# One place in each unit for ScalarE's part of a weight conversion, and an earlier Newton step, in an attention and two-MoE kernel

## The chip, the cores and the metric

The kernel runs on one core of one Trainium2 chip. The metric is the device time of one execution in microseconds. Before the change the median of three runs is 876.39 us (876.0 to 878.66).

## What is computed

The reference chains three layers. First comes attention over 4 batches of 8 heads, 576 positions and head size 64, in which a position sees itself and the 63 positions in front of it. Then a gated layer over the 2304 tokens (512 features, 1536 hidden), with a root-mean-square norm in front of it. Last comes a layer of eight experts, of which each token takes the one with the largest gate.

```python
rms = np.sqrt(np.mean(x * x, axis=-1, keepdims=True) + 1e-06)
xn = x / rms * rms_g
g = xn @ w_gate
silu = g * (1.0 / (1.0 + np.exp(-g)))
val = xn @ w_val
return (silu * val @ w_out).astype(np.float32)
```

The arrays `w_gate`, `w_val` and `w_out` of the second layer come to the chip in float64, because dividing by a NumPy float64 scalar turns them into that type. The kernel brings them to float32 on the chip; this conversion is what the change is about.

## The kernel before

**Stages.** In the page's times: attention to about 130 us, the gated layer to about 600 us, the experts behind it. All five engines run through written-out instruction streams, in the order in which the Python program issues them (`manual_schedule`); nothing is reordered afterwards. Each engine works its stream in order, and waits where an operand isn't ready.

**The gated layer.** Its weights are cut into 12 columns `f` of 128 hidden features (`wraw[f]`, 1536 numbers in each partition: 512 of gate, 512 of value, 512 of out). The tokens are cut into blocks (`BLOCKS`); the first has two sub-blocks of 384 tokens. A *unit* `u` is one column with one sub-block, so the first block has units 0 to 23: an even unit and the odd one behind it share a column, but for units 0 to 3. For each unit TensorE makes gate and value (`gate_val`, 48 matmuls into two banks), and then the output product of the unit before (`out_b`, 9 matmuls). ScalarE makes the silu of the gate into `t` (L642), VectorE multiplies it by the value (L643), ScalarE casts the product to the high half `hh` (L644), and the low half `hl` is a subtraction, on GpSimd in the first block (L645). The banks of gate and value are the same two for all units from 2 on, so that the next unit's gate needs this unit's L642, and its value this unit's L643. Every matrix is split in such a way into a high and a low half of float32r, and each product is three matmuls.

**Weights of a unit.** `w_split` casts a column's high half on ScalarE (L546) and subtracts for the low half (L548). For gate and value (`wha`, `wla`) this is done two units ahead of an even unit, with the subtraction on VectorE; for the out part (`who`, `wlo`) one unit ahead, in an odd unit, with the subtraction on GpSimd.

**The conversion.** `w_conv` turns a column of float64 into float32 in two *halves* of 768 numbers; half `i` belongs to column `i // 2`. A DMA (L389, `w_load`) brings the words of a half into one of three buffers `st`. For halves from 4 on, the steps are:

- ScalarE, `inside(i)`: the sign and the range of each number in `gt` (two buffers), by L458 and L459.
- ScalarE, `scaled(i)`: the high word times 65536 into the place of the result in `wraw`, L466.
- VectorE: shift and mask in place (L427), the low word's bits put in (L432), and the minimum with the largest float32 and the product with the sign (L440).

Half `i` must be through before the cast of its column. `w_conv` is a generator that yields its estimated cost; `beside` runs pieces of it, of the norms and of later work behind each unit until that unit's budget (`BUDGET`) is used up, and `convert` makes it run on where a column is needed. In the kernel before, VectorE's piece of half `i` issues ScalarE's two steps of half `i + 1` between L432 and L440 (`if i + 1 in st_t:`), so that ScalarE works ahead; the first two pairs of `inside` are issued in two of the last steps of attention (`if g in (NG + 1, NG + 2) and w64`).

**The norms.** `norm(i)` prepares the tokens of sub-block `i`: a DMA of the attention's output into `xr` (L323), squares on ScalarE (L332), sums (L337), a sum over partitions on TensorE (`ones`), three Newton steps for the inverse root (each is a square on ScalarE, L355, and L357 and L359 on VectorE), and for four chunks a scaling (L366, VectorE), a cast (L368, ScalarE) and a subtraction (L371, VectorE) into `xt`. Norm 1 belongs to the second sub-block, used from unit 2 on; norms 2 and later belong to the next blocks and run beside the units of the first.

**The end of attention.** In the steps behind the last group of heads, ScalarE and VectorE copy the last results out of their banks (L248, L249). Unit 1 takes two of these banks.

**SyncE's queue** issues all the loads above in program order, together with eight writes of 1 MB that fill `xs` for the experts, one in every second unit from unit 2 on (L916).

Of the kernel before, what the change touches and what calls it, by code (L numbers as in the profile page):

```python
# [22 lines left out]
NF = FF // 128  # L23
# [27 lines left out]
def attention_moe_moe_kernel(ctx, tc, qT, kT, vw, w1p, rms_g, wg2, wg2T, w2p, out):  # L51
# [67 lines left out]
    w64 = w1p.dtype != F32  # L119
# [52 lines left out]
    NG = NU * 3  # L172
# [101 lines left out]
    def beside(tasks, budget):  # L274

        for t in tasks:
            t.rest = 0.0
        while budget > 0:
            can = [t for t in tasks if not t.done and t.rest <= 0 and t.want != "bank"
                   and not (callable(t.want) and not t.want())]  # L280
            if not can:
                break
            cost = can[0].piece()
            budget -= cost
            for o in tasks:
                if o is not can[0]:
                    o.rest -= cost
        return budget
# [88 lines left out]
    st_t, freed = {}, []  # L377
# [13 lines left out]
    def w_conv(f):  # L391


        for h in range(2):
            if not w64:
                w_load(2 * f + h + 3)
                continue
            i = 2 * f + h
            gt = inside(i)
            wf = half(i)  # L400
            w = wf.bitcast(I32)
            if f < 2:
                st = st_t.pop(i)
                lo, hi = st[:, :, 0], st[:, :, 1]
                nc.vector.tensor_scalar(out=w, in0=hi, scalar1=3, scalar2=0x3FFFFFFF,
                                        op0=ALU.logical_shift_left, op1=ALU.bitwise_and)
                yield 0.55
                while freed:
                    w_load(freed.pop())
                nc.vector.scalar_tensor_tensor(out=w, in0=lo, scalar=29, in1=w,  # L410
                                               op0=ALU.logical_shift_right, op1=ALU.bitwise_or)
                yield 1.0
                nc.vector.scalar_tensor_tensor(out=w, in0=hi, scalar=-0x40000000, in1=w,
                                               op0=ALU.bitwise_and, op1=ALU.bitwise_or)
                yield 1.0
                if i + 1 in st_t and i < 3:
                    inside(i + 1)
                del in_t[i]
                yield "rest"
                nc.vector.scalar_tensor_tensor(out=wf, in0=gt, scalar=TINY64 * TINY64, in1=wf,  # L420
                                               op0=ALU.is_ge, op1=ALU.mult)
                yield 0.9
            else:
                scaled(i)
                yield 0.0
                lo = st_t.pop(i)[:, :, 0]
                nc.vector.tensor_scalar(out=w, in0=w, scalar1=3, scalar2=0x7FFFFFFF,  # L427
                                        op0=ALU.logical_shift_left, op1=ALU.bitwise_and)
                yield 0.6
                while freed:  # L430
                    w_load(freed.pop())
                nc.vector.scalar_tensor_tensor(out=w, in0=lo, scalar=29, in1=w,  # L432
                                               op0=ALU.logical_shift_right, op1=ALU.bitwise_or)
                yield 1.2
                if i + 1 in st_t:
                    inside(i + 1)
                    scaled(i + 1)
                del in_t[i]
                yield "rest"
                nc.vector.scalar_tensor_tensor(out=wf, in0=wf, scalar=FMAX, in1=gt,  # L440
                                               op0=ALU.min, op1=ALU.mult)
                yield 1.0
            freed.append(i + 3)

    in_t, sc_t = {}, set()

    def half(i):
        return wraw[i // 2][:, i % 2 * HW:(i % 2 + 1) * HW]
# [1 line left out]
    def inside(i):  # L450

        if i not in in_t:
            gt = in_t[i] = gt_p.tile([P, HW], F32, name="gt")
            hi = st_t[i][:, :, 1].bitcast(F32)
            if i < 4:
                nc.scalar.activation(gt, hi, AF.Square, scale=1.0)
            else:
                nc.scalar.activation(gt.bitcast(I32), hi, AF.Copy, scale=0.49 / TINY64)  # L458
                nc.scalar.activation(gt, gt.bitcast(I32), AF.Sign, scale=1.0)  # L459
        return in_t[i]  # L460

    def scaled(i):

        if i not in sc_t:
            sc_t.add(i)
            nc.scalar.activation(half(i), st_t[i][:, :, 1].bitcast(F32), AF.Copy, scale=65536.0)  # L466
# [85 lines left out]
    for g in range(NG + LV):  # L552
        if g == NG:
            early.finish()
            norm0.finish(bank[2])
        if g < NG:
            if g % 3 == 0:
                qk_load(g // 3 + 2)
            if g % 3 == 2:
                v_load(g // 3 + 1)  # L560
            scores(g)
        if 0 <= g - LT < NG:
            transposes(g - LT)
        if 0 <= g - LV < NG:
            pv(g - LV)
        if g >= NG:
            for _ in range(2):
                next(first_gv, None)
        if 0 <= g - LT < NG:
            pt_copy(g - LT)  # L570
        if 0 <= g - 2 < NG:
            normalise(g - 2)
        attending_work(g)
        if g < NG:
            softmax(g)
        if 0 <= g - LV < NG:
            xo_out(g - LV)
        if 0 <= g - 1 < NG:
            guard(g - 1)
        if g in range(G_LOAD, G_LOAD + 5, 2):  # L580
            w_load((g - G_LOAD) // 2)
        if g == 1:
            nc.sync.dma_start(table.rearrange("(p a) w -> p (a w)", p=P), fill.rearrange("p a w -> p (a w)"))
            nc.sync.dma_start(x2dram[NT:NT + 1], zrow)
        if g == NG - 1:

            nc.scalar.activation(warm, warm, AF.Silu, scale=1.0)
        elif g == NG:
            rest1 = w_split(1, ("b", 1), wraw[1], 1024, {"a": nc.gpsimd}, "a")
        elif g == NG + 1:  # L590
            for _, r in rest1:
                r()
        if g in (NG + 1, NG + 2) and w64:
            inside(g - NG + 3)
    for _ in first_gv:
        pass
    actx.close()
    attending[0] = False

# [293 lines left out]
    for u, (k, i) in enumerate(units):  # L893
        n = steps[k][0]
        first, last = (i == steps[k][2][x] for x in (0, -1))
        begin = u == starts[blocks[n][2][0]]
        gate_val(u)
        silu(u)
        budget = BUDGET[n] + min(spare, 0.5)

        if len(blocks[n][2]) > 1:
            bk = bank[1]
        else:
            bk = bank[4] if n == len(blocks) - 1 else bank[5]
        if u > 0:
            out_b(u - 1)
        if not (begin and len(blocks[n][2]) == 1):
            budget -= on_bank(bg, bk)
        if u > 0:
            budget -= evac(u - 1)  # L910
        if u == stops[i]:
            free[0] = i + 1
        if u in range(2, 2 + 2 * E, 2):

            e = u // 2 - 1
            nc.sync.dma_start(xs[e * NT:e * NT + 4 * P], x2dram[NT:NT + 1].to_broadcast([4 * P, DM]))  # L916
        rest = b_split(heads[u + 1], "o") if u + 1 in heads else []
        if u + 2 in heads:
            rest += b_split(heads[u + 2], "a")
        elif u + 2 >= len(units):  # L920
            rest += c_split(u + 2 - len(units), True)
        if conv.done and wg_bc is None:
            right.close()
            g_p, r_p, j_p = (pool(x, b, right, side="right") for x, b in (("g", 1), ("r", 2), ("j", 2)))
            wg_bc = g_p.tile([P, E, DM], F32, name="wg_bc")
            nc.sync.dma_start(wg_bc, wg2T.partition_broadcast(P))
        budget -= sum(c for c, _ in rest)
        spare = beside([norm1, conv] + bg, budget)
        for _, r in rest:
            r()  # L930
        if n == len(blocks) - 1 and last:

            while c_next < NRING and (c_next + 1) * W2B <= (NF + 2 + k - len(steps)) * WB:
                c_load(c_next)
                c_next += 1
        if u + 3 in heads:
            spare -= convert(max(f for _, f, _ in steps[:heads[u + 3] + 1]) + 1, conv)
        if u + 1 < len(units):
            while normed[0] < units[u + 1][1]:
                late = normer if norm1.done else norm1  # L940
                late.piece(bk if late.want == "bank" else None)
        bg = [t for t in bg if not t.done]
# [257 lines left out]
```

## Time and profile before

| what | value |
|---|---|
| median of three runs | 876.39 us |
| the profiled execution by itself | 877.93 us |
| its span, first to last instruction | 876.1 us |
| mean granted TensorE clock | 0.992 of full speed |
| TensorE matmul busy | 838.9 us, 96% |
| TensorE weight loads busy | 772.7 us, 88% |
| VectorE busy | 605.1 us, 69% |
| ScalarE busy | 449.7 us, 51% |
| GpSimd busy | 203.1 us, 23% |

The profile is one execution on the chip. Engines are PE (TensorE matmuls), PEld (its weight loads), DVE (VectorE), ACT (ScalarE), POOL (GpSimd) and SP (SyncE, DMA issue). Times in the rows are in us from the start of the span; L57 is the helper that issues every matmul. The shares are means over the whole span, so a stage must be looked at by itself.

### The profile page before, as it was taken

How to read it: one execution, taken by the hardware profiler on the slowest of the kernel's cores; microseconds unless marked ns; L12 is line 12 of the kernel's file. 1: busy time of each engine (PE TensorE's matmuls, PEld its weight loads, DVE VectorE, ACT ScalarE, POOL GpSimd, SP SyncE). 2: the span in 40 equal slices, each digit the busy share in tenths (PEclk: the TensorE clock that was granted, in tenths of full speed). 3: DMA queues.
4: the chain of work that ended last, by engine and by line, in shares of the span. 5: the costliest groups of instructions: out<-in, count | busy, mean ns of one | idle time of the engine just before them, and what ended most of it. 6: DMA issues, size and time to landing. Idle time of an engine off the chain costs nothing.

```text
span 876.1 us, 13526 instructions
## 1 busy us (share of the span) xinstructions
PE 838.9 (96%) x4667; PEld 772.7 (88%) x4667; DVE 605.1 (69%) x1472; ACT 449.7 (51%) x993; POOL 203.1 (23%) x227
## 2 busy tenths in 40 slices
PE   7999987999999999999999999999999999989995
PEld 7999986899999999999999999988888898878884
DVE  6789877677975667675578854697775756655463
ACT  5787786776754334222334333335655655554452
POOL 3348573322332000000500041005200121022011
PEclk9999999999999999999999999999999999999998
DMA  7988615999732210000220016424774565462010
GB/s 215 301 268 266 202 67 152 240 236 218 186 87 106 98 36 1 1 0 1 82 64 1 1 49 204 169 97 150 220 254 155 192 217 168 169 210 74 2 45 20
DMA packets 47071, 114.49 MB, mean 131 GB/s; under 512 B 10223, under 2 KB 14703, under 8 KB 46834
## 3 DMA queue, kind: packets, MB, share of 16 engines
q1 hardware_dynamic: 42386, 103.50, 38.7%
q0 software_dynamic: 4576, 9.47, 2.9%
q8 instruction: 77, 1.26, 0.6%
q14 instruction: 32, 0.26, 0.1%
HBM read 93.90 MB, written 31.10 MB: 143 GB/s over the span
## 4 chain that ended last, share of the span: by engine, by line
PE 73%; DVE 9%; issue 7%; DMA 4%; ACT 3%; POOL 2%; SPq 0%; POOLq 0%; DVEq 0%; ACTq 0%
PE bank L57 70%; DMA out_dram<-x,ix 3%; DVE junk L708 2%; DMA st<-in_w1p_dram 1%; PE bank L226 1%; PE bank L849 1%; DVE wla L548 1%; POOL wraw L221 1%; DVE t L643 1%; DVE sm L208 1%; ACT gt L458 1%; DVE wlo L548 0%; POOL out_dram L1019 0%; DVE wraw L432 0%; DVE wraw L230 0%
## 5 line engine op out<-in xcount | busy, mean ns | idle before, releaser
L57 PE MATMUL bank<-xt,wha 128*128 128x384 f32 (+3 forms) x1728 | 421.6, 328 | 18.2 <-issue 6.6
L57 PEld LDWEIGHTS bank<-xt,wha 128*128 128x128 f32 x1728 | 305.1, 189 | 34.9 <-issue 7.9
L57 PE MATMUL bank<-xt,wla 128*128 128x384 f32 (+3 forms) x864 | 281.2, 326 | 0.7 <-DVE wla L548 0.7
L57 PEld LDWEIGHTS bank<-xt,wla 128*128 128x128 f32 x864 | 163.6, 189 | 2.3 <-DVE wla L548 1.7
L57 PE MATMUL bank<-who,hl 128*128 128x512 f32 x384 | 151.8, 395 | 0.6 <-DVE hl L1003 0.6
L57 PE MATMUL bank<-wlo,hh 128*128 128x512 f32 x384 | 151.9, 396 | 0.0
L57 PE MATMUL bank<-who,hh 128*128 128x512 f32 x384 | 151.2, 394 | 0.4 <-ACT hh L644 0.2
L644 ACT CAST hh<-t 128x384 fp32r<-128x384 f32 x72 | 37.0, 513 | 149.6 <-DVE t L643 149.6
L548 DVE TENSOR_TENSOR wla<-wraw,wha 128x512 fp32r<-128x512 f32 (+1 forms) x112 | 98.9, 883 | 5.1 <-ACT wha L546 4.6
L1003 DVE SCALAR_TENSOR_TENSOR hl<-bank,hh 128x512 fp32r<-128x512 f32 (+1 forms) x72 | 45.3, 629 | 82.3 <-ACT hh L1002 82.1
L643 DVE TENSOR_TENSOR t<-t,bank 128x384 f32<-128x384 f32 x72 | 39.8, 553 | 85.0 <-PE bank L57 75.7
L1002 ACT ACTIVATE hh<-bank 128x512 fp32r<-128x512 f32 (+1 forms) x72 | 39.7, 551 | 99.4 <-PE bank L57 99.3
L57 PEld LDWEIGHTS bank<-who,hl 128*128 128x128 f32 x384 | 72.3, 188 | 17.4 <-DVE hl L1003 1.4
L546 ACT CAST wha<-wraw 128x512 fp32r<-128x512 f32 (+1 forms) x113 | 87.0, 770 | 0.0
L1019 POOL DMA_INDIRECT out_dram<-x,ix x32 | 34.9, 1091 | 217.8 <-ACT x L1018 210.8
L57 PEld LDWEIGHTS bank<-who,hh 128*128 128x128 f32 x384 | 72.8, 189 | 12.1 <-issue 0.5
L57 PEld LDWEIGHTS bank<-wlo,hh 128*128 128x128 f32 x384 | 72.6, 189 | 11.1
L57 PE MATMUL bank<-kt,qz 128*128 128x128 f32 x288 | 76.3, 405 | 5.4 <-DMA kt<-in_kT_dram 4.7
L546 ACT CAST who<-wraw 128x512 fp32r<-128x512 f32 x111 | 68.7, 619 | 20.6 <-PE bank L57 20.5
L57 PEld LDWEIGHTS bank<-kt,qz 128*128 128x128 f32 x288 | 72.4, 334 | 6.0 <-issue 4.7
L708 DVE SCALAR_TENSOR_TENSOR junk<-x,wg_bc 128x512 f32<-128x512 f32 x120 | 75.9, 686 | 0.0
L548 DVE TENSOR_TENSOR wlo<-wraw,who 128x512 fp32r<-128x512 f32 x99 | 68.1, 688 | 11.0 <-ACT who L546 6.3
(162 smaller groups left out, 959.9 us busy)
## 6 DMA issues: line engine op xcount, KB each, us to landing
wraw<-in_w2p_dram SPq DMA_DIRECT2D x64, 512.0 KB, 4.4
st<-in_w1p_dram SPq DMA_DIRECT2D x24, 768.0 KB, 6.7
wraw<-in_vw_dram SPq DMA_DIRECT2D x16, 512.0 KB, 4.4
xs<-x2dram SPq DMA_DIRECT2D x8, 1024.0 KB, 11.7
qz<-in_qT_dram SPq DMA_DIRECT2D x32, 144.0 KB, 5.5
xdram<-wraw SPq DMA_DIRECT2D x16, 288.0 KB, 2.3
x2dram<-x SPq DMA_DIRECT2D x18, 256.0 KB, 2.9
kt<-in_kT_dram SPq DMA_DIRECT2D x15, 288.0 KB, 5.9
```

Of the source, the lines that this page charges most:

```text
L57: nc.tensor.matmul(o, l, r, start=start, stop=stop)
L208: nc.vector.tensor_tensor_reduce(out=sm[:, j], in0=sb[:, j * P:(j + 1) * P], in1=mask[:, 0 if i0 + j == 0 else 1], scale=-0.125, scalar=3. ...
L221: nc.gpsimd.tensor_tensor(out=p, in0=p, in1=rs.unsqueeze(2).to_broadcast([P, 3, P]), op=ALU.mult)
L226: nc.tensor.transpose(bank[3 + g % 2][:, j * P:(j + 1) * P], p[:, j], ident)
L546: nc.scalar.copy(wh, src[:, r])
L548: e.tensor_tensor(out=wl, in0=src[:, r], in1=wh.bitcast(F32), op=ALU.subtract)))
L643: nc.vector.tensor_tensor(out=t, in0=t, in1=v, op=ALU.mult)
L644: nc.scalar.copy(hh[:, :nt], t)
L708: nc.vector.scalar_tensor_tensor(out=junk, in0=x2, scalar=1.0, in1=wg_bc[:, e], op0=ALU.mult, op1=ALU.mult, accum_out=lg[:, j, e:e + 1])
L1002: nc.scalar.activation(hh[:, :n], bank[k % 2][:, :n], AF.Relu, scale=1.0)
L1003: nc.vector.scalar_tensor_tensor(out=hl[:, :n], in0=bank[k % 2][:, :n], scalar=0.0, in1=hh[:, :n].bitcast(F32), op0=ALU.max, op1=ALU.subtract)
L1019: d = nc.gpsimd.indirect_dma_start(out=out[:, :], in_=y, in_offset=None, out_offset=bass.IndirectOffsetOnAxis(ap=ix[:, j, 0:1], axis=0), b ...
```

## The change

The diff is whole.

```diff
--- before.py
+++ after.py
@@ -396,6 +396,8 @@
                 w_load(2 * f + h + 3)
                 continue
             i = 2 * f + h
+            if f >= 2:
+                yield lambda: i in sc_t
             gt = inside(i)
             wf = half(i)
             w = wf.bitcast(I32)
@@ -432,17 +434,21 @@
                 nc.vector.scalar_tensor_tensor(out=w, in0=lo, scalar=29, in1=w,
                                                op0=ALU.logical_shift_right, op1=ALU.bitwise_or)
                 yield 1.2
-                if i + 1 in st_t:
-                    inside(i + 1)
-                    scaled(i + 1)
                 del in_t[i]
-                yield "rest"
                 nc.vector.scalar_tensor_tensor(out=wf, in0=wf, scalar=FMAX, in1=gt,
                                                op0=ALU.min, op1=ALU.mult)
+                halves[0] = i + 1
                 yield 1.0
             freed.append(i + 3)
 
-    in_t, sc_t = {}, set()
+    in_t, sc_t, halves = {}, set(), [4]
+
+    def ahead():
+
+        i = next((i for i in range(halves[0], 2 * NF) if i not in sc_t), 2 * NF)
+        if w64 and i < min(halves[0] + 2, 2 * NF) and i in st_t:
+            scaled(i)
+            inside(i)
 
     def half(i):
         return wraw[i // 2][:, i % 2 * HW:(i % 2 + 1) * HW]
@@ -585,15 +591,16 @@
         if g == NG - 1:
 
             nc.scalar.activation(warm, warm, AF.Silu, scale=1.0)
+            if w64:
+                inside(4)
         elif g == NG:
             rest1 = w_split(1, ("b", 1), wraw[1], 1024, {"a": nc.gpsimd}, "a")
         elif g == NG + 1:
             for _, r in rest1:
                 r()
-        if g in (NG + 1, NG + 2) and w64:
-            inside(g - NG + 3)
     for _ in first_gv:
         pass
+    beside([norm1], 1.2)
     actx.close()
     attending[0] = False
 
@@ -925,6 +932,10 @@
             wg_bc = g_p.tile([P, E, DM], F32, name="wg_bc")
             nc.sync.dma_start(wg_bc, wg2T.partition_broadcast(P))
         budget -= sum(c for c, _ in rest)
+        if u == 0 and w64:
+            scaled(4)
+        elif n == 0:
+            ahead()
         spare = beside([norm1, conv] + bg, budget)
         for _, r in rest:
             r()
```

ScalarE's two steps of a half are no longer issued by VectorE's piece of the half before. A new function `ahead` issues them for the next half that has not had them, once in each unit of the first block, behind the unit's weight cast and in front of the pieces that `beside` runs; the words are scaled first now, and the sign comes second. VectorE's piece of a half does not start before its `scaled` has been issued. The first pair of `inside` is issued with the table load in the last step of attention, the second goes into unit 1, and half 4's `scaled` into unit 0. Behind the loop of attention a call of `beside` runs the last Newton step of norm 1 before the first silu is issued.

In the changed file the line numbers are others: `inside` is L464 and L465, `scaled` L472, VectorE's three steps L429, L434 and L438, the split L552 and L554, and silu, product and cast of `hh` are L649, L650 and L651.

ScalarE at the end of attention and in units 0 and 1, before (`wraw5` is the second sub-block's attention output here, `bank6` and `bank7` are the banks that unit 1 takes):

```order
L248 COPY wraw5_113<-bank5_70 64x192
L249 COPY wraw5_113<-bank5_70 64x192
L458 ACTIVATE gt_1531<-st_1066 128x768
L459 ACTIVATE gt_1531<-gt_1531 128x768
L249 COPY wraw5_113<-bank6_71 64x192
L355 ACTIVATE wraw4_112<-wraw4_112 128x384
L248 COPY wraw5_113<-bank7_72 64x192
L249 COPY wraw5_113<-bank7_72 64x192
L546 CAST who0_1564<-wraw0_108 128x512
L642 ACTIVATE t_1587<-bank0_65 128x384
L644 CAST hh_1588<-t_1587 128x384
L546 CAST who1_1566<-wraw0_108 128x512
```

and with the change:

```order
L355 ACTIVATE wraw4_112<-wraw4_112 128x384
L248 COPY wraw5_113<-bank5_70 64x192
L249 COPY wraw5_113<-bank5_70 64x192
L249 COPY wraw5_113<-bank6_71 64x192
L355 ACTIVATE wraw4_112<-wraw4_112 128x384
L248 COPY wraw5_113<-bank7_72 64x192
L249 COPY wraw5_113<-bank7_72 64x192
L552 CAST who0_1563<-wraw0_108 128x512
L649 ACTIVATE t_1586<-bank0_65 128x384
L651 CAST hh_1587<-t_1586 128x384
L552 CAST who1_1565<-wraw0_108 128x512
L472 ACTIVATE wraw1_109<-st_897 128x768
```

The pair L458, L459 in front of the copy out of `bank6` is gone, and `scaled` of half 4 (L472) stands behind the cast of `who1`.

ScalarE in units 7 and 8 of the first block, before (`st_1927` and `st_1980` hold the words of halves 12 and 13):

```order
L642 ACTIVATE t_1961<-bank0_65 128x384
L644 CAST hh_1962<-t_1961 128x384
L546 CAST who0_1564<-wraw2_110 128x512
L458 ACTIVATE gt_1983<-st_1927 128x768
L459 ACTIVATE gt_1983<-gt_1983 128x768
L466 ACTIVATE wraw3_111<-st_1927 128x768
L642 ACTIVATE t_2016<-bank0_65 128x384
L644 CAST hh_2017<-t_2016 128x384
L546 CAST wha0_130<-wraw2_110 128x1024
L458 ACTIVATE gt_2037<-st_1980 128x768
L459 ACTIVATE gt_2037<-gt_2037 128x768
L466 ACTIVATE wraw3_111<-st_1980 128x768
```

and with the change:

```order
L651 CAST hh_1959<-t_1958 128x384
L552 CAST who0_1563<-wraw2_110 128x512
L472 ACTIVATE wraw2_110<-st_1873 128x768
L464 ACTIVATE gt_1976<-st_1873 128x768
L465 ACTIVATE gt_1976<-gt_1976 128x768
L355 ACTIVATE sq_1714<-sq_1714 128x384
L649 ACTIVATE t_2012<-bank0_65 128x384
L651 CAST hh_2013<-t_2012 128x384
L552 CAST wha0_130<-wraw2_110 128x1024
L472 ACTIVATE wraw3_111<-st_1927 128x768
L464 ACTIVATE gt_2031<-st_1927 128x768
L465 ACTIVATE gt_2031<-gt_2031 128x768
```

The words `st_1927` of half 12 are taken up in unit 8 (behind the cast of `wha0`), where before it was in unit 7, and L472 stands in front of L464 and L465. A Newton square (L355) of norm 2 has come in front of the silu of unit 8.

VectorE in the same units, from the end of unit 7 to the product of unit 9, before:

```order
L357 TENSOR_TENSOR sq_1657<-sq_1657 128x384
L359 SCALAR_TENSOR_TENSOR sq_1657<-sq_1657 128x384
L440 SCALAR_TENSOR_TENSOR wraw2_110<-wraw2_110,gt_1930 128x768
L427 TENSOR_SCALAR wraw3_111<-wraw3_111 128x768
L643 TENSOR_TENSOR t_2016<-t_2016,bank1_66 128x384
L432 SCALAR_TENSOR_TENSOR wraw3_111<-st_1927,wraw3_111 128x768
L548 TENSOR_TENSOR wla0_131<-wraw2_110,wha0_130 128x1024
L643 TENSOR_TENSOR t_2067<-t_2067,bank1_66 128x384
```

and with the change:

```order
L357 TENSOR_TENSOR sq_1714<-sq_1714 128x384
L359 SCALAR_TENSOR_TENSOR sq_1714<-sq_1714 128x384
L650 TENSOR_TENSOR t_2012<-t_2012,bank1_66 128x384
L429 TENSOR_SCALAR wraw3_111<-wraw3_111 128x768
L434 SCALAR_TENSOR_TENSOR wraw3_111<-st_1927,wraw3_111 128x768
L438 SCALAR_TENSOR_TENSOR wraw3_111<-wraw3_111,gt_2031 128x768
L357 TENSOR_TENSOR sq_1714<-sq_1714 128x384
L359 SCALAR_TENSOR_TENSOR sq_1714<-sq_1714 128x384
L554 TENSOR_TENSOR wla0_131<-wraw2_110,wha0_130 128x1024
L650 TENSOR_TENSOR t_2066<-t_2066,bank1_66 128x384
```

In both orders half 12 (`st_1927`, into `wraw3`) belongs to unit 8, but all three of its steps and a Newton step now lie between the product of unit 8 and the subtraction for `wla0`; before, its first step stood ahead of that product, and its last behind the next one.

The rows of TensorE are the same in both orders, but for the norm's sum over partitions of a later block, which is taken two units earlier. On SyncE, the load of norm 2's `xr` stood behind one load of `st` after the last output of attention; now it is behind three, with one write of `xs` between them. GpSimd's rows are the same.

## Rows read from the trace of the kernel before

**Rows 1.** Busy us by stretch: length, PE, PEld, DVE, ACT, POOL; clock, DMA share, GB/s.
```profile
130.00:165.00 35.00, 28.01 (x139) 23.93 (x139) 22.72 (x32) 23.25 (x40) 8.98 (x7) 1.00 0.66 172
...
156.45:259.87 103.42, 102.12 (x534) 94.53 (x533) 80.62 (x97) 74.92 (x115) 34.43 (x25) 1.00 0.79 202
```

**Rows 2.** Timeline of PE, first matmul of unit 1; start, us, instruction, idle before.
```profile
132.30 0.62 PE L57 MATMUL bank<-xt,wha 128*128 128x384 f32 x2 [2.10 <-ACT wraw L249]
```

**Rows 3.** Timeline of ACT, end of attention.
```profile
130.13 0.90 ACT L458 ACTIVATE gt<-st 128x768 int32<-128x768 f32 x1
...
131.93 0.32 ACT L249 COPY wraw<-bank 64x192 f32<-64x192 f32 x1
```

**Rows 4.** Timeline of DVE, end of attention to unit 1.
```profile
130.55 0.34 DVE L248 COPY wraw<-bank 64x192 f32<-64x192 f32 x1
134.64 0.56 DVE L643 TENSOR_TENSOR t<-t,bank 128x384 f32<-128x384 f32 x1 [3.75 <-ACT t L642]
...
137.29 2.06 DVE L366 SCALAR_TENSOR_TENSOR wraw<-wraw,gs_sb,wraw 128x384 f32<-128x384 f32 x2
...
142.93 0.55 DVE L371 TENSOR_TENSOR xt<-wraw,xt 128x384 fp32r<-128x384 f32 x1
```

**Rows 5.** Timeline of ACT, units 3 to 5.
```profile
158.63 1.76 ACT L332 ACTIVATE sq<-xr 128x384 f32<-128x384 f32 x4
...
164.69 0.51 ACT L644 CAST hh<-t 128x384 fp32r<-128x384 f32 x1 [0.62 <-DVE t L643]
165.11 1.04 ACT L546 CAST wha<-wraw 128x1024 fp32r<-128x1024 f32 x1
166.06 0.89 ACT L458 ACTIVATE gt<-st 128x768 int32<-128x768 f32 x1
166.98 0.85 ACT L459 ACTIVATE gt<-gt 128x768 f32<-128x768 int32 x1
167.73 0.90 ACT L466 ACTIVATE wraw<-st 128x768 f32<-128x768 f32 x1
...
171.40 0.62 ACT L546 CAST who<-wraw 128x512 fp32r<-128x512 f32 x1
```

**Rows 6.** Timeline of DVE, a conversion in unit 1, and the split in unit 12.
```profile
144.38 0.69 DVE L427 TENSOR_SCALAR wraw<-wraw 128x768 int32<-128x768 int32 x1 [0.90 <-ACT wraw L466]
...
146.97 0.56 DVE L427 TENSOR_SCALAR wraw<-wraw 128x768 int32<-128x768 int32 x1
147.56 0.96 DVE L432 SCALAR_TENSOR_TENSOR wraw<-st,wraw 128x768 int32<-128x768 int32 x1
148.55 0.96 DVE L440 SCALAR_TENSOR_TENSOR wraw<-wraw,gt 128x768 f32<-128x768 f32 x1
...
220.25 1.22 DVE L548 TENSOR_TENSOR wla<-wraw,wha 128x1024 fp32r<-128x1024 f32 x1
221.38 0.55 DVE L643 TENSOR_TENSOR t<-t,bank 128x384 f32<-128x384 f32 x1
```

**Rows 7.** Timeline of DVE, the products of units 4 and 20.
```profile
164.10 0.56 DVE L643 TENSOR_TENSOR t<-t,bank 128x384 f32<-128x384 f32 x1 [2.79 <-ACT t L642]
...
264.76 0.55 DVE L643 TENSOR_TENSOR t<-t,bank 128x384 f32<-128x384 f32 x1
```

**Rows 8.** Timelines of DVE and of POOL, unit 7.
```profile
184.61 1.94 DVE L432 SCALAR_TENSOR_TENSOR wraw<-st,wraw 128x768 int32<-128x768 int32 x1
...
184.12 1.62 POOL L548 TENSOR_TENSOR wlo<-wraw,who 128x512 fp32r<-128x512 f32 x1
```

**Rows 9.** Groups by line, DVE, 156 to 260 us; busy, mean ns, idle before.
```profile
L427 DVE TENSOR_SCALAR wraw<-wraw 128x768 int32<-128x768 int32 x17 | 13.5, 796 | 2.7 <-ACT wraw L466 2.7
```

**Rows 10.** Busy time by stretch, experts, columns as in rows 1.
```profile
745.00:750.00 5.00, 2.88 (x16) 2.33 (x15) 2.58 (x4) 2.21 (x4) 0.70 (x1) 0.92 0.87 322
750.00:755.00 5.00, 5.00 (x29) 4.59 (x28) 1.91 (x4) 2.21 (x4) 0.00 (x0) 0.74 0.14 50
```

**Rows 11.** DMA issues; line, KB each, us to landing.
```profile
xs<-x2dram SPq DMA_DIRECT2D x8, 1024.0 KB, 11.7
```

## The prediction, made before the run

> **What bounds the kernel now.** Read the stretches first [rows 1]: from 130 to 165 us, where the expert stage opens, TensorE works 28.0 of 35.0 us; from 156.45 to 259.87 us, units 4 to 19 of the first block, it works 102.1 of 103.4. So the second stretch is TensorE's own, and the only time that an earlier ScalarE can win here lies in the 7.0 us of gaps before it. The largest is read next [rows 2]: the first matmul of unit 1 stood 2.10 us, released by ScalarE's copy at line 249. On ScalarE's time line that copy sits right behind a pair of conversion instructions, L458 and L459 [rows 3]; its partner on VectorE was done 1.0 us earlier [rows 4].
>
> The third reading is the one that decides. In units 4 to 19 VectorE does one half of a weight conversion in each unit (L427, L432, L440), on words that ScalarE put there (L466) with a sign (L458, L459). L427 ran 17 times there, and the idle time in front of all of them together was 2.7 us, behind L466 [rows 9]. ScalarE had done its share one unit ahead. And VectorE is busy 80.6 of the 103.4 us [rows 1]: it has 1.4 us a unit to give away, no more.
>
> **The change, part by part.** No instruction is added or removed on any engine; the orders change.
>
> *Opening.* Both sign pairs leave the copies of the last attention units: one goes ahead to the table load, where ScalarE stood idle, the other into unit 1. The copy at 131.93 then waits for VectorE's copy instead, which ends at 130.89 [rows 4] and can itself move up a little, since the Newton step in front of it needs ScalarE too. That makes 1.0 to 1.5 us; I take 1.5 for the copy, the first silu and the first product (L643, called the product below), which goes from 134.64 to 133.1. The Newton step that followed this product is now ahead of it, so that the first L366 follows 0.9 us behind instead of 2.65. From there to the end of the last L371 the chain took 6.2 us, from 137.29 to 143.48 [rows 4], then comes one L427 (0.6), and product 1 falls at 133.1 + 0.9 + 6.2 + 0.6 = 140.8. Before product 2 VectorE must do five conversion instructions of halves 4 and 5, at the starts of rows 6 (0.59, 0.99, 0.87) some 5.5 us with one wait on GpSimd: 146.3. Two more steps, by the loop that follows: product 3 at 152.9; and behind it ScalarE has the sign pair and four squares of 1.76 us [rows 5] in front of silu 4, so 6.4 us: product 4 at 159.3. Before it was at 164.10 [rows 7]. The opening brings 4.8 us. Bounds: 0 if a later wait eats it, 7.0 if every gap went.
>
> *The loop.* Now ScalarE does L466 of half u+4 in unit u behind the weight cast, and VectorE needs that very half at once, behind the product of unit u. So each unit contains a round trip: product, cast of hh, weight cast, L466, L427. From rows 5, counted from the start of a product: hh cast 0.59, weight cast 1.01, L466 1.96 (it takes the place that L458 has there), and L427 0.92 after the start of L466, since it started as soon as L466 had ended [rows 6], so 2.9. The product itself keeps VectorE 0.5 us; for the other 2.4 us VectorE stands, every even unit. L432 follows at 3.5; the sign is ready at 4.5 (L458 0.8 behind L466, L459 0.92 behind that, 0.85 long), L440 at 4.6, L548 0.9 later, the next product 1.13 behind that [rows 6]: 6.6 us. In odd units the weight cast is 0.62 instead of 1.04 [rows 5] and there is no L548: L427 at 2.5, L440 at 4.15, the next product at 5.0.
>
> In odd units GpSimd's two subtractions run just when L427 wants to start. What that costs shows where it happened before: L432 took 1.94 us beside a GpSimd subtraction, and 0.96 alone [rows 8, 6]. I take 0.8 an odd unit, bounds 0 and 1.0. The Trainium skill (SBUF — State Buffer, section SBUF: two separate sides) has the two engines share a port pair as an exclusive lock, held for a whole instruction by whoever starts first. By that L427 would wait to the end of GpSimd's instruction, which is the upper bound rather than a shared slowdown; the row's 0.98 us lost agrees, and with a halved price the sum below would be 3 us lower.
>
> So a pair of units takes 6.6 + 5.0 + 0.8 = 12.4 us. Before, 16 units took 264.76 − 164.10 = 100.7 us from product to product [rows 7], 12.6 a pair. The bare loop just fits. But the second block's norm lies in it too: between product 4 and product 20 the changed order has on VectorE 24 instructions of the norms (six sums, five Newton steps of two, eight of scaling and splitting) at 0.53 us, as the L371 of rows 4 less its overlap, and two short ones: 13.4 us. Before, these lay in VectorE's spare time; now that time is spent on standing, and they lengthen the loop. Three times a silu stands behind a Newton square or a cast that waits for the last of them (units 7, 11, 17): half a microsecond for that and half for the silu, 3 x 1.07 = 3.2 us. Sum: 8 x 12.4 + 13.4 + 3.2 = 115.8 us, against 100.7: **15.1 us lost**.
>
> *SyncE's queue.* The load of the second norm's input moves from behind one load of weights to behind three and a 1 MB write of `xs`. Such a write took 11.7 us from issue to landing [rows 11]. By the times above the load is issued near 145.5 and wanted at 157: about hidden; 0 to 3 us, taken as 0. The loads of weights themselves are wanted one unit later than before, which costs nothing.
>
> *Sum.* −4.8 + 15.1 = +10.3 us. From unit 20 on nothing of this is left, and the blocks behind it have the same order on all engines, so the shift stays. The profiled execution took 877.93 us by itself (span 876.1); that gives 888.2. The median of the runs is 1.5 us below it: **886.7 us**.
>
> **The rivals.**
> 1. *It fits, and the opening is kept: faster.* The change adds no work, and neither helper engine is full: VectorE 78%, ScalarE 72% in units 4 to 19 [rows 1]. If the stands of L427 fall wholly into VectorE's idle 22.8 us, TensorE stays the bound and the gain is 4.8 to 7.0 us: 869.4 to 871.6. It decides at 12.6 us a pair, norm included; the loop above has 14.5. The Trainium skill (Perfetto Trace Analysis, section Identifying the Most-Contended Engine) judges these engines by occupancy and puts the work on the fullest one. By that rule this rival wins; the rows speak against it, because the idle time is spread while the round trip comes in series with the work. 13%.
> 2. *GpSimd holds nothing up.* Then 6.4 us less: 880.3. For it: which of the two engines starts first decides, and where VectorE is first it is GpSimd that waits, with time to spare. Against it: rows 8, where VectorE came second. 13%.
> 3. *The clock falls.* The forecast puts stands of one to three microseconds in front of TensorE in most units. Late in the trace the granted clock was 0.92 in a stretch in which TensorE worked 2.88 of 5 us and 0.74, between 1.2 and 2.4 GHz, in the next [rows 10]: 0.4 + 1.3 = 1.7 us lost. Against it: after the 2.10 us stand at 130 us the clock stayed at 1.00 [rows 1]. Two or three such falls: 890 to 892. 7%.
> 4. *Loss and gain cancel*: the round trip costs only half of what I take. Within 2.6 us of 876.4. 9%.
>
> **How the numbers follow.** The forecast itself (883 to 889.5) gets 58%. About 0.3%, 2.6 us, is what a measurement of this kernel can tell from no change. Faster is rival 1: 0.13. Same is rival 4: 0.09. Slower is the rest: 0.78. The range reaches over rivals 2 and 3 and the bounds of the lock and the load: 877.5 to 892; what it leaves out is rival 1, part of rival 4 and the top of rival 3.
>
> **What would show it.** Right: L427 (line 429 there) waits for L466 in nearly every unit, some 35 to 45 us in sum where it was 2.7; TensorE's gap before unit 1 falls from 2.1 to some 0.6 us; product 4 near 159 and product 20 near 275; from unit 4 TensorE has gaps of 1 to 3 us released by `wla` or by a silu. The opening is wrong if product 4 is later than 162. The loop is wrong if pairs without norm work take over 13 us, or if TensorE stays above 98% in units 4 to 19: then rival 1 holds. The lock is wrong if odd units show no L427 that starts as a GpSimd instruction ends.

## The result, and the profile after

The changed kernel takes 890.33 us (median of six runs, 887.27 to 893.69), against 878.51 us for the kernel before in the same comparison: ratio 1.0139, with an interval of 1.0108 to 1.017. It is slower by 11.8 us; the forecast was 10.3 us slower, 886.7 us. The profiled execution took 892.58 us (span 890.8, mean clock 0.986).

Busy time by stretch, the changed kernel, the same two stretches and columns as [rows 1]:

```profile
130.00:165.00 35.00, 30.28 (x149) 26.69 (x148) 22.98 (x32) 22.98 (x40) 9.32 (x8) 0.97 0.71 188
...
156.45:259.87 103.42, 93.83 (x464) 84.59 (x463) 67.50 (x88) 64.65 (x101) 23.05 (x21) 0.97 0.78 193
```

The opening gained: TensorE works 30.3 us of the first 35, up from 28.0. The stretch that TensorE had filled to 99% now has 9.6 us of gaps, and VectorE and ScalarE are both less busy than before. Nothing became full; engines wait for one another.

Timeline of PE at unit 1, then of DVE at products 4 and 20 (rows 2 and 7 before):

```profile
130.71 0.62 PE L57 MATMUL bank<-xt,wha 128*128 128x384 f32 x2 [0.60 <-ACT wraw L249]
```

```profile
161.28 0.56 DVE L650 TENSOR_TENSOR t<-t,bank 128x384 f32<-128x384 f32 x1 [2.94 <-ACT t L649]
...
277.13 0.55 DVE L650 TENSOR_TENSOR t<-t,bank 128x384 f32<-128x384 f32 x1
```

The stand before unit 1 fell from 2.10 to 0.60 us. Product 4 came 2.8 us earlier than before, product 20 12.4 us later: 115.85 us between them, where it had been 100.7. TensorE's gaps in between add up to 8.7 us; its busy time there is 6.6 us longer than before, at a mean granted clock of 0.97.

Groups by line, DVE, units 4 to 19, as [rows 9]:

```profile
L429 DVE TENSOR_SCALAR wraw<-wraw 128x768 int32<-128x768 int32 x16 | 15.8, 987 | 30.7 <-ACT wraw L472 30.7
```

Each of the 16 conversions begins with a wait for ScalarE's share. Two units show the round trip, first on ACT, then on DVE (product 8 falls at 190.03, product 9 at 197.65, product 10 at 203.50):

```profile
190.62 0.51 ACT L651 CAST hh<-t 128x384 fp32r<-128x384 f32 x1 [0.62 <-DVE t L650]
191.03 1.05 ACT L552 CAST wha<-wraw 128x1024 fp32r<-128x1024 f32 x1
191.98 0.89 ACT L472 ACTIVATE wraw<-st 128x768 f32<-128x768 f32 x1
192.78 0.89 ACT L464 ACTIVATE gt<-st 128x768 int32<-128x768 f32 x1
193.70 0.85 ACT L465 ACTIVATE gt<-gt 128x768 f32<-128x768 int32 x1
```

```profile
192.91 0.56 DVE L429 TENSOR_SCALAR wraw<-wraw 128x768 int32<-128x768 int32 x1 [2.33 <-ACT wraw L472]
193.50 0.96 DVE L434 SCALAR_TENSOR_TENSOR wraw<-st,wraw 128x768 int32<-128x768 int32 x1
194.58 0.96 DVE L438 SCALAR_TENSOR_TENSOR wraw<-wraw,gt 128x768 f32<-128x768 f32 x1
...
200.10 1.42 DVE L429 TENSOR_SCALAR wraw<-wraw 128x768 int32<-128x768 int32 x1 [1.90 <-ACT wraw L472]
```

In the even unit L429 runs 2.9 us behind the product's start, right behind L472; L438 waits for the sign that ends at 194.55. In the odd unit L429 takes 1.42 us instead of 0.56, and ends 0.41 us behind GpSimd's subtraction for `wlo`, which runs until 201.11. On POOL:

```profile
199.81 1.30 POOL L554 TENSOR_TENSOR wlo<-wraw,who 128x512 fp32r<-128x512 f32 x1
```

One loss had been forecast as nothing, within bounds of 0 to 3 us. Timeline of ACT in unit 3, and SP:

```profile
159.11 1.76 ACT L332 ACTIVATE sq<-xr 128x384 f32<-128x384 f32 x4 [2.62 <-DMA xr<-xdram]
```

```profile
145.36 1.76 SPq L323 DMA_DIRECT2D xr<-xdram  x1
```

The squares began 13.7 us after the load of `xr` was issued at 145.36; ScalarE stood 2.62 us for it, with silu 4 behind.

### The profile page after: what moved, and what is told of

Read it like the earlier page. It is cut to its first block, busy times and chain, and to the rows that moved or that the text cites. A ratio compares the mean times of both kernels' runs of the same rounds, so it can differ in the third digit from the quotient of the medians.

```text
span 890.8 us, 13539 instructions
## 1 busy us (share of the span) xinstructions
PE 845.8 (95%) x4667; PEld 776.1 (87%) x4667; DVE 599.0 (67%) x1472; ACT 448.8 (50%) x993; POOL 194.6 (22%) x227
## 4 chain that ended last, share of the span: by engine, by line
PE 63%; DVE 13%; issue 8%; ACT 7%; DMA 5%; POOL 2%; SPq 0%; DVEq 0%; POOLq 0%; ACTq 0%
PE bank L57 61%; DMA out_dram<-x,ix 3%; DMA xr<-xdram 2%; DVE junk L715 2%; DVE wla L554 1%; DVE wraw L438 1%; ACT wraw L472 1%; PE bank L226 1%; DVE wraw L429 1%; DVE t L650 1%; ACT hh L651 1%; PE bank L856 1%; DVE wraw L434 1%; ACT wha L552 1%; ACT who L552 1%
## 5 line engine op out<-in xcount | busy, mean ns | idle before, releaser
L57 PEld LDWEIGHTS bank<-xt,wha 128*128 128x128 f32 x1728 | 307.0, 191 | 39.0 <-ACT t L649 11.3
L651 ACT CAST hh<-t 128x384 fp32r<-128x384 f32 x72 | 36.9, 513 | 156.5 <-DVE t L650 156.5
L554 DVE TENSOR_TENSOR wla<-wraw,wha 128x512 fp32r<-128x512 f32 (+1 forms) x112 | 98.1, 876 | 3.8 <-ACT wha L552 3.3
L650 DVE TENSOR_TENSOR t<-t,bank 128x384 f32<-128x384 f32 x72 | 39.8, 552 | 72.6 <-PE bank L57 56.5
L552 ACT CAST wha<-wraw 128x512 fp32r<-128x512 f32 (+1 forms) x113 | 87.1, 770 | 0.0
L1030 POOL DMA_INDIRECT out_dram<-x,ix x32 | 34.9, 1090 | 218.6 <-ACT x L1029 211.6
L552 ACT CAST who<-wraw 128x512 fp32r<-128x512 f32 x111 | 68.7, 619 | 21.2 <-PE bank L57 20.1
L554 DVE TENSOR_TENSOR wlo<-wraw,who 128x512 fp32r<-128x512 f32 x99 | 68.2, 689 | 12.0 <-ACT who L552 5.5
```

Of the source, the lines that this page charges most:

```text
L57: nc.tensor.matmul(o, l, r, start=start, stop=stop)
L552: nc.scalar.copy(wh, src[:, r])
L554: e.tensor_tensor(out=wl, in0=src[:, r], in1=wh.bitcast(F32), op=ALU.subtract)))
L650: nc.vector.tensor_tensor(out=t, in0=t, in1=v, op=ALU.mult)
L651: nc.scalar.copy(hh[:, :nt], t)
L1030: d = nc.gpsimd.indirect_dma_start(out=out[:, :], in_=y, in_offset=None, out_offset=bass.IndirectOffsetOnAxis(ap=ix[:, j, 0:1], axis=0), b ...
```

## The experiments

The theory T: ScalarE, one unit late, puts a round trip into each unit. Rivals: VectorE simply overfull (R1), and the late `xr` load with clock falls (R2). The table gives three products in us, each from one profile, and the ratio to the kernel before as it was measured beside each run.

| run | product 4 | product 20 | product 23 | ratio [interval] |
|---|---|---|---|---|
| before | 164.10 | 264.76 | 283.12 | 1 |
| changed | 161.28 | 277.13 | 294.43 | 1.0139 [1.0108, 1.017] |
| after_again | 161.63 | 277.52 | 294.82 | 1.0141 [1.0106, 1.0175] |
| lead | 161.60 | 268.00 | 286.80 | 1.002 [0.9996, 1.0045] |
| loop | 160.32 | 276.33 | 293.65 | 1.0085 [1.0062, 1.0108] |
| opening | 160.74 | 264.88 | 283.68 | 0.9997 [0.997, 1.0024] |
| xr_early | 158.63 | 274.51 | 291.81 | 1.0075 [1.0045, 1.0104] |
| scaled_first | 161.50 | 275.55 | 293.12 | 1.0113 [1.0079, 1.0147] |
| pool_cut | 161.51 | 276.26 | 293.69 | 1.0128 [1.01, 1.0157] |
| opening_step | 160.92 | 261.59 | 279.95 | 0.9959 [0.994, 0.9978] |
| lead_step | 161.94 | 264.02 | 282.17 | 0.9988 [0.9965, 1.0011] |
| best | 162.23 | 262.74 | 280.89 | 0.9966 [0.9945, 0.9987] |
| best_xs | 159.19 | 259.78 | 277.93 | 0.9944 [0.9917, 0.997] |

**lead: ScalarE one unit ahead again, all else in its place.**

```diff
-                yield lambda: i in sc_t
+                yield lambda: i <= unit[0] + 4
...
             ahead()
+            if u == 2:
+                ahead()
```

> The changed kernel with one thing more: in unit 2 ScalarE does its share for two halves, so that from then on it is one unit ahead of VectorE again; VectorE's, TensorE's and SyncE's orders are as in the changed kernel. Theory T (the round trip product, cast of hh, weight cast, L472, L429 inside one unit is what costs the 15 us): the wait of VectorE's first step for ScalarE falls from 30.7 us in units 4 to 19 to under 4, product 4 to product 20 takes 101 to 103 us instead of 115.9, and the time is 874 to 878 us. Rival R1 (VectorE is simply overfull, its steps and GpSimd's lock fill the units, the waits only move): the wait falls but the lock and the steps stay, product 4 to 20 stays above 111, time 886 to 891. Rival R2 (the late load of xr and the two falls of the clock behind the stands are the larger part): they stay, 884 to 888.

Measured: 879.46 us beside 879.06 before. Up to 230 us it went as T says. Two of the groups on DVE from 155 to 240 us; then busy time from 156.45 to 230 of this run and of the changed kernel:

```profile
L438 DVE SCALAR_TENSOR_TENSOR wraw<-wraw,gt 128x768 f32<-128x768 f32 x13 | 20.9, 1607 | 0.4
...
L429 DVE TENSOR_SCALAR wraw<-wraw 128x768 int32<-128x768 int32 x12 | 6.7, 556 | 0.0
```

```profile
156.45:230.00 73.55, 71.65 (x376) 66.41 (x376) 58.98 (x70) 54.52 (x84) 29.68 (x17) 1.00 0.79 209
```

```profile
156.45:230.00 73.55, 65.73 (x321) 59.38 (x320) 46.39 (x61) 44.22 (x70) 15.74 (x15) 0.95 0.79 191
```

With the same VectorE order the wait is zero, and from product 4 to product 15 it took 69.1 us (before 68.6, changed 80.2). VectorE gets busier and TensorE fuller: R1 falls. The load of `xr` is as late here (product 4 at 161.60), and most of the loss is gone: this speaks against R2 too. But product 4 to 20 took 106.4 us instead of 101 to 103, and the time missed the expected 874 to 878, above all because of one place, on ACT in unit 15 and on SP:

```profile
237.91 0.89 ACT L472 ACTIVATE wraw<-st 128x768 f32<-128x768 f32 x1 [5.61 <-DMA st<-in_w1p_dram]
```

```profile
224.07 0.38 SPq L323 DMA_DIRECT2D xr<-xdram  x1
224.49 0.51 SPq L924 DMA_DIRECT2D xs<-x2dram  x1
225.11 1.23 SPq L389 DMA_DIRECT2D st<-in_w1p_dram  x2
```

Norm 3's load of `xr`, waiting for its buffer, stood in SyncE's queue with a write of `xs` and words behind it; all of them were issued together, from 224.07 on. In the changed kernel the queue bunches in the same way, from 234.90 on, but ScalarE wants these words later and does not wait for them.

**loop: the change without its opening.**

```diff
-            if w64:
-                inside(4)
...
+        if g in (NG + 1, NG + 2) and w64:
+            inside(g - NG + 3)
...
-    beside([norm1], 1.2)
```

> The change without its opening: sign pairs back between the copies of the last attention units, no Newton step ahead of the first silu; ScalarE's one place in each unit stays. Theory T: the loop alone costs about 15 us between products 4 and 20; the squares of norm 2 fall one unit later here than before, so 13 to 16 us over the kernel before: 889 to 894 us. Rival (the loss needs the new opening, since that puts three loads and a write in front of the load of xr): 876 to 882.

Measured: 885.81 us, 6.7 above before. Product 4 to 20 takes 116.0 us, L429 waits 29.9 us: the loop needs no new opening to be slow, and the rival falls. Product 4 came at 160.32 without the opening's edits: the squares of norm 2, in unit 3 before, fall into unit 4 here. That doesn't explain why the total lies below the expected range: at product 23 the shift is 10.5 us, which would be 889.6. The difference arises behind product 23 (see the end of the next section).

**opening, and opening_step.** The first is the change's opening alone on the kernel before; the second adds one line that issues norm 3's load of `xr` a unit later.

```diff
             nc.scalar.activation(warm, warm, AF.Silu, scale=1.0)
+            if w64:
+                inside(4)
...
-        if g in (NG + 1, NG + 2) and w64:
-            inside(g - NG + 3)
...
+    beside([norm1], 1.2)
```

```diff
     def norm(i):
+        if i == 3:
+            yield "step"
```

> The change's opening alone, on the kernel before: one sign pair goes to the table load, the other is issued by the conversion, the Newton step goes ahead of the first silu; ScalarE is issued ahead by VectorE's piece as before. Theory T: the gap of TensorE before unit 1 falls from 2.1 to about 0.6 us, 3 to 5 us are won by product 4 and kept, since in the loop ScalarE works ahead: 873 to 876 us. Rival (a later wait eats the opening): 877 to 880.

> The run opening (the change's opening alone on the kernel before) with norm 3's load of xr issued one unit later, so that a load of words stands ahead of it in SyncE's queue. Theory T (the opening is worth 3.4 us at product 4, and in the run opening it was given back in unit 15, where ScalarE waited 5.2 us for words that were queued behind that load): the wait goes, product 20 at 261 to 262.5 instead of 264.88, product 23 some 3 us before the kernel before's 283.12, time 2 to 4 us under it. Rival (the words were late for the DMA engines' sake, whatever the queue's order): product 20 at 264 or later, no difference to before.

Measured: 876.89 us beside 879.06 before, ratio 0.9997, so no difference; and 874.68 us beside 878.81, faster. Product 4 falls 3.4 us earlier in opening; at product 20 this is gone. Norm 2's work has moved up too (its squares run in unit 2, at 151.58), and with it norm 3's load of `xr`, issued at 221.54 where it was at 231.60. On ACT in unit 15 of opening:

```profile
236.32 0.90 ACT L458 ACTIVATE gt<-st 128x768 int32<-128x768 f32 x1 [5.25 <-DMA st<-in_w1p_dram]
```

With the queue's order mended product 20 falls at 261.59 and the gain stays. So the opening was worth its 3 us, and a load that was in nobody's way before took it back; the rival of the first run was right in what happens, that of the second wrong.

**xr_early: the changed kernel with norm 2's load right behind attention's last write.**

```diff
...
     attending[0] = False
+    pre.append(big(0))
+    xr_load(pre[0], *subs[2][:2])
```

> The changed kernel with norm 2's load of xr issued right behind attention's last write, ahead of the three loads of words and the write of xs; every other order is the same. Theory T: ScalarE's wait of 2.62 us before the squares goes, and with it TensorE's stand of 2.58 us before unit 5 and the fall of the clock behind it (1.7 us): product 4 at 158.5 to 159.5, and 2 to 4.5 us less than the changed kernel, 886 to 888.5 us. Rival (another wait takes its place, words of halves 5 to 7 arrive later): no difference, within 1 us of the changed kernel. If most of the loss were here (rival R2), 880 or less.

Measured: 886.03 us. In unit 3 on ACT:

```profile
156.48 1.75 ACT L340 ACTIVATE sq<-xr 128x384 f32<-128x384 f32 x4
```

The wait is gone, product 4 comes at 158.63, 2.65 us earlier, and the gain is still 2.6 us at product 23. That is the price of the queue's order in the profiles; the ratios, 1.0075 and 1.0139, are further apart. Had most of the loss been here, the time would have been 880 or less, so R2 falls.

**after_again: the changed kernel once more.**

> The changed kernel once more, on the chip of this call, as the base for the two runs beside it: 888 to 891 us, L429 waiting some 31 us in units 4 to 19 and 115.9 us from product 4 to product 20, with stands and clock falls at the same places if they come from the order, elsewhere if by chance.

Measured: 889.78 us, with L429 waiting 30.7 us and 115.89 us from product 4 to 20: it repeats. One thing didn't. Busy time from 220 to 225 us, of the changed kernel and of this run:

```profile
220.00:225.00 5.00, 4.77 (x18) 4.77 (x19) 2.28 (x4) 4.35 (x7) 1.01 (x1) 0.66 0.16 66
```

```profile
220.00:225.00 5.00, 4.44 (x25) 4.44 (x26) 2.07 (x3) 4.35 (x8) 1.03 (x1) 1.00 0.23 95
```

The first had a granted clock of 0.66 here, the second 1.00, each behind a stand of TensorE of 2.8 us, and product 12 to 13 took 7.06 and 7.05 us. Here, where TensorE is not last, the fallen clock cost nothing.

**scaled_first: L472 in front of the weight cast.**

```diff
...
+        if 0 < u and n == 0 and w64:
+            early_scaled()
         rest = b_split(heads[u + 1], "o") if u + 1 in heads else []
```

> The changed kernel with ScalarE's L472 in front of the weight cast instead of behind it; the sign pair stays behind the cast. Theory T (the round trip counts by its last link: in an even unit the sign, at 4.5 us, sets L438 anyway, in an odd unit GpSimd's subtractions no longer end last): the wait of L429 falls by 8 x 0.95 + 8 x 0.5, some 10 to 12 us, but product 4 to 20 only by 0 to 6.4. Rival (each microsecond of L429's wait is a microsecond of the loop): 10 to 12 us less, 104 to 106.

Measured: 886.63 us. Groups on DVE, 155 to 272 us (units 4 to 19, and the end of an L429 of unit 3):

```profile
L434 DVE SCALAR_TENSOR_TENSOR wraw<-st,wraw 128x768 int32<-128x768 int32 x16 | 23.3, 1459 | 0.6
L438 DVE SCALAR_TENSOR_TENSOR wraw<-wraw,gt 128x768 f32<-128x768 f32 x16 | 15.3, 958 | 8.7 <-ACT gt L469 7.8
L429 DVE TENSOR_SCALAR wraw<-wraw 128x768 int32<-128x768 int32 x17 | 11.2, 661 | 20.9 <-ACT wraw L476 20.9
```

L429's wait fell by 9.8 us, the time from product 4 to 20 by 1.8. The wait reappears as L438 standing for the sign (7.8 us) and as L434 held up by GpSimd (1459 ns, 958 in the changed kernel). The largest wait in the list is not the price here; the last link is.

**pool_cut: GpSimd's subtraction for `wlo` in two halves.**

```diff
-            rests.append((..., lambda ...: e.tensor_tensor(out=wl, ...)))
+                for a in range(0, n, m):
+                    e.tensor_tensor(out=wl[:, a:a + m], ...)
```

> The changed kernel with GpSimd's subtraction for wlo as two instructions of 256 columns instead of one of 512; the same numbers. Theory T, with the lock held for a whole instruction: in odd units L429 arrives 0.3 us after wlo has started and waits to its end, 1.41 us instead of 0.56; with the halves it waits to the end of the first, about 0.45 instead of 0.85 us, so L429 at about 1.0 in odd units and 8 x 0.4 = 3 us less from product 4 to 20, if the second half does not take the port back from L434. Rival (GpSimd only slows the engines' shared access down): no difference, L429 stays at 1.4.

Measured: 889.19 us, ratio 1.0128, which can't be told from the changed kernel's. Unit 9, on DVE and on POOL:

```profile
200.06 0.87 DVE L429 TENSOR_SCALAR wraw<-wraw 128x768 int32<-128x768 int32 x1 [1.90 <-ACT wraw L472]
200.96 1.38 DVE L434 SCALAR_TENSOR_TENSOR wraw<-st,wraw 128x768 int32<-128x768 int32 x1
```

```profile
199.77 1.76 POOL L555 TENSOR_TENSOR wlo<-wraw,who 128x256 fp32r<-128x256 f32 x2
```

L429 ends 0.6 us earlier, and L434 then takes 1.38 us instead of 0.96, while the second half runs beside it. From product 4 to 20, 1.1 us are left of the 3 us expected. In these rows access changes hands between GpSimd's two instructions.

**lead_step, best, best_xs: mending the queue too.** All three have ScalarE ahead and norm 3's load a unit later; best also has norm 2's load early, best_xs instead the writes of `xs` four units later:

```diff
-        if u in range(2, 2 + 2 * E, 2):
+        if u in range(6, 6 + 2 * E, 2):
...
-            e = u // 2 - 1
+            e = u // 2 - 3
```

> The run lead with the same edit alone: norm 3's load of xr one unit later, norm 2's load left where the change has it. Theory T: ScalarE's wait of 5.61 us in unit 15 goes, product 4 at 161.6 as in lead, product 16 at 236 to 237.5 instead of 240.87, product 20 at 261.5 to 263, and 1 to 3 us less than the kernel before. Rival: the wait stays, product 20 at 266 or later.

> The changed kernel with three things more: ScalarE one unit ahead from unit 2 on (as in the run lead), norm 2's load of xr issued right behind attention's last write, and norm 3's load of xr issued one unit later, behind the next load of words. Theory T, as the run lead extended it (the round trip is the loop's cost; what was left over there is SyncE's queue, in which norm 3's load of xr, waiting for its buffer, held up the words of half 20 until ScalarE stood 5.61 us for them): both stands go; product 4 at 158.5 to 159.5, product 20 at 259 to 262 where before it was 264.76, and 3 to 6 us less than the kernel before: 873 to 876 us. Rival (another stand takes the place of this one, since words and xs share the DMA engines): product 20 at 264 or later, 877 to 880.

> The run lead_step with the eight writes of xs in units 6, 8, ... 20 instead of 2, 4, ... 16. Theory: in units 2 to 4 the xs writes and the loads share the DMA engines; the load of xr took 13.7 us from issue to the squares in the changed kernel, 4.4 is its usual time. Without them xr lands before 155, product 4 at 158.5 to 159.5, product 20 at 259.5 to 261.5: 3 to 6 us less than the kernel before, and 0 to 3 less than the run best. Rival (the writes only move the collision to units 18 to 20, or the squares wait for something else): product 4 at 161 or product 23 above 282.

Measured: 877.29, 874.54 and 873.75 us, beside 878.81, 877.54 and 878.81 before. In lead_step the 5.61 us in unit 15 went, but product 20 came later than expected (264.02), and the gain can't be told from none. In best the time came as expected, product 4 (162.23) and product 20 (262.74) did not: `xr` was in time, but ScalarE, one unit ahead, stood for words in unit 3, as it had in lead (2.19 us) and lead_step (2.25 us):

```profile
157.61 0.90 ACT L482 ACTIVATE wraw<-st 128x768 f32<-128x768 f32 x1 [2.79 <-DMA st<-in_w1p_dram]
```

In best_xs neither is late: the load of `xr`, issued at 145.13, landed after 7.7 us, where it took 13.7 us in lead. Unit 3 on ACT, and the long stretch of rows 1:

```profile
157.04 1.75 ACT L334 ACTIVATE sq<-xr 128x384 f32<-128x384 f32 x4
```

```profile
156.45:259.87 103.42, 103.42 (x543) 96.38 (x543) 82.94 (x100) 72.02 (x112) 43.28 (x25) 1.00 0.86 210
```

TensorE is busy throughout. This version beats both kernels, by 0.56% and, taking the two ratios together, by about 2% (0.9944 / 1.0139).

## Why the prediction was right

*The sum.* The forecast was 10.3 us; the profiles show 12.4 at product 20 and 11.3 at product 23, the medians 11.8. The measured 890.33 us lies just above the 883 to 889.5 that the prediction held most likely, and inside its wider range of 877.5 to 892. The loop was foreseen; the other terms were less exact than the total. (The stretch from 130 to 165 us, which the prediction calls the opening of the expert stage, is that of the gated layer.)

*The loop* was right in mechanism and size: 115.8 us forecast, 115.85 measured. Its parts hold too, though a match to 0.05 us is luck. An even unit without norm work takes 6.56 us (products 2 to 3; forecast 6.6), an odd one 5.83 to 5.85 (5 to 6, 9 to 10; forecast 5.0 + 0.8). L429's wait in units 4 to 19 is 30.7 us, below the 35 to 45 named beside the 2.7 of the same units before; over the whole block it is 34.9. In the three units where the forecast put a silu behind a norm step (products 8, 12 and 18) VectorE stood 0.97 us for it each time. The gaps of 1 to 3 us in TensorE are rarer than forecast: between products 4 and 20 three exceed 1 us (2.58, 2.77 and 1.41).

*Rival 1* (it fits) fell by the run lead: with the serial wait taken away the same work fits, so no engine was overfull. By the rule that the prediction quoted from the Trainium skill (Perfetto Trace Analysis, Identifying the Most-Contended Engine) TensorE would have stayed the bound; here occupancy of 78% and 72% on the helpers did not show that their idle time lies in a chain.

*The lock* was right at 0.8: 1.42 against 0.56 us for L429 in an odd unit. Rival 2 fell. The sign that the prediction named, a start as a GpSimd instruction ends, isn't there in that form: the row has L429 start at 200.10, run long, and end just behind GpSimd's end at 201.11. The rule in the Trainium skill (SBUF — State Buffer, SBUF: two separate sides) of a lock held for a whole instruction agrees with pool_cut, where cutting the instruction shortened L429 and lengthened its successor.

*SyncE's queue* is the step that was mis-sized: taken as 0 within bounds of 0 to 3, it cost 2.65 us (xr_early). The forecast had the load issued near 145.5, and it was, at 145.36; it then took 13.7 us to the squares, beside words and a write of `xs`. That is why product 4 fell at 161.28 and not at 159.3; products 0 to 3 fell within about 0.5 us of the forecast, always earlier.

*The opening* was the sum's weakest term. Product 4 came 2.8 us earlier (5.5 with the queue mended) where 4.8 was forecast. Opening and loop alone bring it forward by 3.4 and 3.8 us, but norm 2's squares lie ahead of product 3 in the one and behind product 4 in the other, so these don't add. And the gain doesn't reach the end: at product 23 the loop alone stands at 293.65, the changed kernel with its opening at 294.43, and the opening alone at 283.68 where the kernel before has 283.12. In both cases a load of `xr` in SyncE's queue took it back; with the queue mended 1.8 us (xr_early beside loop) and 3.2 us (opening_step) are left. So the 4.8 us that the sum credits weren't won; that the total came out near all the same is in part luck.

*Rival 3*: behind stands of TensorE of 2.6 to 2.9 us the clock fell in some places and in others it did not (0.66 and 1.00 in the two rows shown at after_again). Its price of 1.7 us a fall was not paid where VectorE and ScalarE were last: product 4 to 5 took 8.12 us after such a fall, and 8.10 in xr_early, where the clock stayed at 1.00.

Left open: behind product 23 the orders are the same, but the profiled executions differ from there to the end by up to 7.5 us. A part of this goes with the clock. From product 23 to the end, the changed kernel and best, columns as in rows 1:

```profile
294.43:890.70 596.27, 571.30 (x3165) 518.28 (x3163) 384.01 (x829) 254.07 (x458) 81.38 (x102) 0.98 0.30 99
```

```profile
280.89:869.70 588.81, 567.21 (x3165) 514.40 (x3163) 383.86 (x829) 254.33 (x458) 80.42 (x102) 0.99 0.31 100
```

The executions of one kernel differ in the same way: the fastest of after_again, 884.37 us, had a mean granted clock of 0.994, the slowest, 891.87 us, 0.986. The median clock was 0.992 in loop and in xr_early, 0.988 in after_again; so a part of the 4.0 us between the medians of loop and after_again, of which 1.2 us stand at product 23, is likely the clock's. No run tests that.

## What to carry to other kernels

Before a producer is moved closer to its consumer, write down the chain between them for one unit and add its durations: occupancy says whether work fits, only the chain says whether it fits in that order. When a step that issues DMAs moves, read the whole in-order queue for which loads now stand behind one that must wait for its buffer, at the opening and at every later place where the same step recurs. In these runs the removal of a wait brought less than its total (1.8 of 9.8 us in scaled_first, 9.45 of 30.7 in lead, from product 4 to 20); look at what would be last next.

## What was unexpected of the hardware

A load of `xr`, which took 4.4 us as a median in the kernel before, took 13.7 us with a 1 MB write and words around it, and 7.7 us without the write (best_xs). Cutting a GpSimd instruction in two cost 0.46 us more (1.76 against 1.30) and gave VectorE its access earlier, only to take most of it back. Where the contention lands depends on the order: on L429 in the changed kernel (987 ns), on L434 in scaled_first (1459 ns), on L438 in lead (1607 ns), each 0.55 to 0.96 us when undisturbed.
